# Decode attention: K turned by VectorE in 32 by 32 squares of bf16 pairs, products 512 columns wide, one quad of heads per loop turn

## The chip, the cores and the metric

The kernel runs on one core of a Trainium2 chip. The metric is the device time of one execution in microseconds (us). The profile's span, from the first to the last instruction, is about 1.8 us shorter than the time. Engines are called as in the profile: PE is TensorE (PEld its weight loads), DVE is VectorE, ACT is ScalarE, POOL is GpSimd, SP is the engine that issues transfers (SPq its queue). "The clock" is the one granted to TensorE, as a part of the full one.

Here "slow" means over 1.5% above the fastest run of the same kernel. Comparisons below use fast runs, except where a slow one is named as such.

## The reference, cut to what matters

One token goes through attention over a cache of 4096 positions and then a gated MLP. All tensors are bf16.

```python
Hq, Hkv, Sk, Dh = 32, 32, 4096, 128      # every head has its own K and V
q = x_norm @ wq                          # 640 -> 32 x 128
scores = einsum("bhqd,bhkd->bhqk", q, k) * Dh ** -0.5
p = softmax(scores)
o = einsum("bhqk,bhkd->bhqd", p, v) @ wo # 4096 -> 640
h = x + o
h2 = h + (gelu(n @ w_gate) * (n @ w_up)) @ w_down   # n = layernorm(h), 640 -> 1728 -> 640
```

K and V have 33.5 MB each; with the weights, 84.23 MB are read from HBM once per execution. Nothing is used twice.

## The kernel before

Four heads make a quad; a quad's K, and its V, is one tile of 128 partitions (4 heads x 32 rows) by 128 positions by 128 features, 4 MB. The kernel wants the features on the partitions for its score products, so TensorE transposes the 128 blocks of a K tile into PSUM, and VectorE and ScalarE copy them back over K. Then come 128 score products with four columns each, the exponentials, and 128 pv products with four columns each. Two tiles of K and two of V are kept, so a load waits for the use of two quads back. (The parts from several places; cuts are marked.)

```python
def pe_transposes(slot, mark, after):
    ...
        for b in range(GRP):                       # 8 blocks to a PSUM bank
            inst = PE.transpose(tp_b[g % NBANK][:, b*DH:(b+1)*DH], kt[slot][:, g*GRP+b, :], ident[:])
    ...
def pe_scores(slot, half, ready, mark):
    for j in range(half * NB // 2, (half + 1) * NB // 2):
        ...
        inst = PE.matmul(s_ps[half][:, j % (NB // 2), :], lhsT=kt[slot][:, j, :],
                         rhs=q8[:, slot*QH:(slot+1)*QH], start=True, stop=True)
    ...
def pe_pv(slot, half, mark):
    landed(f"v{slot}{'ab'[half]}")
    ...
        inst = PE.matmul(o_ps, lhsT=vt[slot][:, j, :], rhs=e_t[:, j, :], start=(j == 0), stop=(j == NB - 1))
    ...
def load_v(m):
    load_kv("v", m, vt, A_v_cache, m >= SLOTS and pe_at(m - SLOTS, "pv"))
...
for m in range(NQ):                                # the order of transfers
    load_k(m)                                      # the last K in two halves
    if m in (0, 2, 4):
        load_wo(m // 2)
    ...
    load_v(m)
load_wo(TURNS - 1)                                 # last part of wo: after the last V
load("wg", ...); load("wu", ...)                   # then w_down
```

The softmax here doesn't subtract the row's maximum and nothing guards it: scores larger than these inputs give would overflow.

## Time and profile before

| | before |
|---|---|
| time, median of 6 runs | 207.52 us (206.64 to 207.79) |
| span of the profiled run | 205.6 us |
| bytes, share of the transfer engines' span | 84.23 MB, 96.2% |
| PE, DVE, ACT busy | 72%, 36%, 40% |

These are lines of the profile's page: the span, the busy time of each engine with its share and its count of instructions, then the transfers' share in 40 equal slices (tenths, 9 is 90% or more), then the transfer queue with its packets, megabytes and share.

```profile
span 205.6 us, 7384 instructions
...
PE 148.5 (72%) x3409; PEld 138.2 (67%) x3409; DVE 73.6 (36%) x185; ACT 81.5 (40%) x179; POOL 19.1 (9%) x17
...
DMA  7999999999999999999999999999999999999980
...
q1 hardware_dynamic: 3952, 84.23, 96.2%
```

The transfer row is full from the second slice to the last but two, while no engine is busy more than 72% of the time. So transfers set the pace. Only at the end do they stop before the program does: at about 200 us of 205.6.

The chain of waits that ended last, followed back from the last instruction, tells what the end consists of. Its columns are start in us, length in us, and what ran.

```profile
171.35 0.87 PE tp_103 L252 x8
...
186.28 1.87 PE o L278 x64
188.15 0.54 PE tp_106 L300 x2
...
200.25 2.39 PE tp_105 L437 x54
...
202.66 0.33 DVE y_row L682
```

The last quad's transposes start at 171.35, its pv ends at 188.15 (186.28 + 1.87), and the rest of the program takes 17.45 us more. No transfer is in the chain.

The groups of instructions give durations from which the change could be costed: line, engine, operation, names, shape and count, then busy us and mean ns of one, then the idle time before them.

```profile
L278 PE MATMUL o<-ex,big 128*128 128x4 bf16 x1024 | 29.9, 166 | 10.2 <-ACT ex L567 6.3 <-issue 3.9
...
L252 PE MATMUL tp_103<-ident,big 128*128 128x128 bf16 x256 | 25.0, 256 | 11.9 <-PEq L176 11.9
...
L580 DVE COPY big<-tp_106 128x1024 bf16<-128x1024 bf16 x24 | 16.6, 691 | 2.9 <-PE tp_106 L252 2.4
...
L643 DVE STREAM_TRANSPOSE g_col<-tp_103 128x416 f32<-128x416 f32 x1 | 0.6, 605 | 0.0
```

The last of these lines: a DVE transpose of 416 f32 elements per partition takes 0.605 us.

### The profile page before, as it was taken

How to read it: one execution, taken by the hardware profiler on the slowest of the kernel's cores; microseconds unless marked ns; L12 is line 12 of the kernel's file. 1: busy time of each engine (PE TensorE's matmuls, PEld its weight loads, DVE VectorE, ACT ScalarE, POOL GpSimd, SP SyncE). 2: the span in 40 equal slices, each digit the busy share in tenths (PEclk: the TensorE clock that was granted, in tenths of full speed). 3: DMA queues.
4: the chain of work that ended last, by engine and by line, in shares of the span. 5: the costliest groups of instructions: out<-in, count | busy, mean ns of one | idle time of the engine just before them, and what ended most of it. 6: DMA issues, size and time to landing. Idle time of an engine off the chain costs nothing. (4 is left out here: it accounts for less than half of the span.)

```text
span 205.6 us, 7384 instructions
## 1 busy us (share of the span) xinstructions
PE 148.5 (72%) x3409; PEld 138.2 (67%) x3409; DVE 73.6 (36%) x185; ACT 81.5 (40%) x179; POOL 19.1 (9%) x17
## 2 busy tenths in 40 slices
PE   0001859955996499869986997099859989986654
PEld 0000259855996499869986997099759979986422
DVE  4006127400570058005701830058016703842570
ACT  0000136540476138614670755037704671772000
POOL 8200000530000000800000053000000000000000
PEclk9999979955595559955955995569856985995555
DMA  7999999999999999999999999999999999999980
GB/s 255 406 454 414 404 457 424 451 434 411 418 446 403 440 424 446 427 434 414 459 427 414 440 421 434 427 453 421 434 421 453 392 427 456 418 426 430 377 327 1
DMA packets 3963, 84.39 MB, mean 410 GB/s; under 512 B 464, under 2 KB 464, under 8 KB 752
## 3 DMA queue, kind: packets, MB, share of 16 engines
q1 hardware_dynamic: 3952, 84.23, 96.2%
q8 instruction: 8, 0.13, 0.3%
q14 instruction: 3, 0.02, 0.0%
HBM read 84.23 MB, written 0.00 MB: 410 GB/s over the span
## 5 line engine op out<-in xcount | busy, mean ns | idle before, releaser
L278 PE MATMUL o<-ex,big 128*128 128x4 bf16 x1024 | 29.9, 166 | 10.2 <-ACT ex L567 6.3
L278 PEld LDWEIGHTS o<-ex,big 128*128 128x128 bf16 x1024 | 28.5, 103 | 11.5 <-ACT ex L567 7.5
L553 ACT COPY big<-tp_104 128x1024 bf16<-128x1024 bf16 x16 | 16.2, 1012 | 47.8 <-PE tp_104 L252 47.8
L252 PE MATMUL tp_103<-ident,big 128*128 128x128 bf16 x256 | 25.0, 256 | 11.9 <-PEq L176 11.9
L252 PEld LDWEIGHTS tp_103<-ident,big 128*128 128x128 bf16 x256 | 20.4, 118 | 12.4 <-issue 12.4
L252 PE MATMUL tp_104<-ident,big 128*128 128x128 bf16 x256 | 24.4, 251 | 0.0
L580 DVE COPY big<-tp_103 128x1024 bf16<-128x1024 bf16 x24 | 16.5, 688 | 19.6 <-PE tp_103 L252 19.6
L252 PE MATMUL tp_105<-ident,big 128*128 128x128 bf16 x256 | 23.3, 244 | 0.0
L500 POOL COPY wo<-wo_in 128x5120 bf16<-128x5120 bf16 x3 | 13.3, 4449 | 104.8 <-PE a L288 104.8
L252 PE MATMUL tp_106<-ident,big 128*128 128x128 bf16 x256 | 22.7, 240 | 0.0
L252 PEld LDWEIGHTS tp_104<-ident,big 128*128 128x128 bf16 x256 | 20.0, 116 | 0.0
L252 PEld LDWEIGHTS tp_105<-ident,big 128*128 128x128 bf16 x256 | 19.1, 112 | 0.0
L252 PEld LDWEIGHTS tp_106<-ident,big 128*128 128x128 bf16 x256 | 18.7, 110 | 0.0
L265 PE MATMUL sb<-q_77,big 128*128 128x4 bf16 x512 | 14.4, 165 | 4.6 <-issue 4.6
L580 DVE COPY big<-tp_106 128x1024 bf16<-128x1024 bf16 x24 | 16.6, 691 | 2.9 <-PE tp_106 L252 2.4
L553 ACT COPY big<-tp_105 128x1024 bf16<-128x1024 bf16 x16 | 16.2, 1014 | 3.2 <-PE tp_105 L252 3.2
L265 PEld LDWEIGHTS sb<-q_77,big 128*128 128x128 bf16 x512 | 13.7, 97 | 4.8 <-issue 4.8
L567 ACT ACTIVATE ex<-sa 32x64 bf16<-32x64 f32 x32 | 9.8, 305 | 11.4 <-PE sa L265 11.2
L580 DVE COPY big<-tp_105 128x1024 bf16<-128x1024 bf16 x16 | 11.1, 692 | 8.4 <-PE tp_105 L252 8.1
L265 PE MATMUL sa<-q_77,big 128*128 128x4 bf16 x512 | 14.0, 165 | 0.0
L265 PEld LDWEIGHTS sa<-q_77,big 128*128 128x128 bf16 x512 | 13.5, 95 | 0.6
L637 DVE COPY o_raw<-o 128x4 f32<-128x4 f32 x4 | 0.6, 162 | 35.8 <-PE o L278 35.8
(111 smaller groups left out, 112.8 us busy)
## 6 DMA issues: line engine op xcount, KB each, us to landing
big<-in_A_v_cache_dram SPq DMA_DIRECT2D x8, 4096.0 KB, 33.7
big<-in_A_k_cache_dram SPq DMA_DIRECT2D x7, 4096.0 KB, 25.9
big<-in_A_wq_dram SPq DMA_DIRECT2D x1, 5120.0 KB, 15.1
wo_in<-in_A_wo_dram SPq DMA_DIRECT2D x4, 1280.0 KB, 27.0
big<-in_A_k_cache_dram SPq DMA_DIRECT2D x2, 2048.0 KB, 23.7
big<-in_B_w_gate_dram SPq DMA_DIRECT2D x1, 2160.0 KB, 38.8
big<-in_B_w_up_dram SPq DMA_DIRECT2D x1, 2160.0 KB, 44.0
big<-in_B_w_down_dram SPq DMA_DIRECT2D x1, 1280.0 KB, 31.9
```

The lines of the kernel that those rows point to most:

```text
L252: inst = PE.transpose(tp_b[g % NBANK][:, b * DH : (b + 1) * DH], kt[slot][:, g * GRP + b, :], ident[:])
L265: inst = PE.matmul(s_ps[half][:, j % (NB // 2), :], lhsT=kt[slot][:, j, :], rhs=q8[:, slot * QH : (slot + 1) * QH], start=True, stop=True,)
L278: inst = PE.matmul(o_ps, lhsT=vt[slot][:, j, :], rhs=e_t[:, j, :], start=(j == 0), stop=(j == NB - 1))
L500: POOL.tensor_copy(wo_t[:], wo_in[:]).then_inc(S["wo"], 1)
L553: ACT.copy(group(m % SLOTS, g), tp_g[g % NBANK]).then_inc(S["act_pe"], 1)
L567: inst = ACT.activation(e_t[r, cols, i], s_ps[half][r, :, i], AF.Exp, scale=SCALE, accum_out=rs_all[r, half, h : h + 1])
L580: DVE.tensor_copy(group(m % SLOTS, g), tp_g[g % NBANK]).then_inc(S["dve_pe"], 1)
L637: event(DVE.tensor_copy(o_raw[:, HG * turn : HG * turn + QH], o_ps))
```

## The change

Its intent is to take the transposes from TensorE, with their 16 PSUM copies per quad, and to replace many narrow products by few wide ones. VectorE turns K in squares of 32 by 32 elements, and the elements are f32 words, so each carries a pair of bf16. Afterwards the even and odd features of a pair are one word apart, and a score product reads every second bf16 of the turned tile. The query becomes the stationary operand, spread so that one of four heads is hit per group of rows; 32 products of 512 columns give all scores of a quad in one bank. pv also has 512 columns, four products side by side, and four f32 products gather the four results.

The program around it changes too: there are two raw K tiles, one turned K tile and *one* V tile; a loop turn is one quad and finishes it, projection included; the last part of wo is loaded before the last K; the last K comes whole. The core of the diff (cuts marked):

```diff
-    kt = [tile_at(i) for i in range(SLOTS)]
-    vt = [tile_at(SLOTS + i) for i in range(SLOTS)]
+    kr = [part(i * TILE, TILE) for i in range(SLOTS)]
+    vt = part(SLOTS * TILE, TILE).rearrange("p (j d) -> p j d", d=DH)
+    kt = part((SLOTS + 1) * TILE, TILE)
 ...
+    def pe_scores(mark):
+        for c in range(NC):
+            PE.wait_ge(S["kt"], c + 1)
+            for k in range(2):
+                for e in range(2):
+                    ...
+                        lhsT=q_wide[:, 2 * k + e, NC - 1 - c : NC - 1 - c + P],
+                        rhs=kt_at[:, k, c, :, e],
 ...
+    with nc.Fori(0, NQ, engines=(only_pe,)):
+        mark = mark_at("quad")
+        pe_scores(mark)
+        PE.wait_ge(S["act_pe"], 1)
+        pe_totals(t_ps, mark)
+        landed("v")
+        pe_pv(mark)
+        PE.wait_ge(S["act_pe"], 2)
+        pe_outputs(mark)
+        ...
+        pe_project(mark)
 ...
     def load_v(m):
-        load_kv("v", m, vt, A_v_cache, m >= SLOTS and pe_at(m - SLOTS, "pv"))
+        if m > 0:
+            SP.wait_ge(S["pe"], pe_at(m - 1, "pv"))
+        load("v", vt.rearrange("p j d -> p (j d)"), rows_of(A_v_cache, m))
 ...
     for m in range(NQ):
         load_k(m)
-        if m in (0, 2, 4):
+        if m % 2 == 0:
             load_wo(m // 2)
         load_v(m)
-    load_wo(TURNS - 1)
 ...
+    for m in range(NQ):                        # VectorE
+        ...                                    # wait for K of this quad
+        for c in range(NC):
+            DVE.transpose(to[:, c], of[:, c].rearrange("p (j k n) -> p j k n", k=2, n=HP)).then_inc(S["kt"], 1)
+        wait_pe(pe_at(m, "s"))
+        ... DVE.transpose(s_turned[:].rearrange("p j c -> p (j c)"), s_bank[:])
+        ...                                    # wait for totals, outputs, reorder
+        DVE.tensor_copy(o_row[:], r_ps).then_inc(S["dve_pe"], 1)
```

## The prediction

> **What bounds the kernel now.** Transfers. The profile's queue table gives one queue 84.23 MB and 96.2% of the span; the windows view shows about 430 GB/s at a share of 1.00 from 5 to 195 us. Transfers start at about 1.5 us and fade out at 200 us; 5 us of computation follow. The engines have slack in the stream (page: PE 72%, DVE 36%, ACT 40%). The bytes stay, so the change lifts no bound; it can only expose computation. The end is already compute: in the chain of waits, pv of the last quad ends at 188.15 and 17.4 us follow.
>
> **What the change removes.** Per quad 128 PE transposes (0.85 us for 8 at clock 0.5, 0.45 at 1.0), 16 PSUM copies (0.69 us DVE, 1.01 us ACT), and 256 products 4 wide. PE busy should fall to about 90 us, ACT to about 30.
>
> **What it adds, per quad.**
> - Eight DVE transposes of 128x1024 f32. The timeline has 416 elements in 0.61 us and 64 in 0.21, back to back 0.73[...].
> - 32 score products 512 wide. The query products, 512 wide and four side by side, take 0.427 us a group at the cold clock; warm I take 0.215.[...]. So PE catches up with DVE and ends about 1.2 us after it.
> - One 0.71 us score transpose, four exponentials of 0.36+0.20 us (2.4), totals 0.55, pv in 8 groups 1.7 to 3.4, ACT copy 0.59, four f32 products (about 1.5), then o_col, spread, reorder, o_row, q_to (about 1.2).
>
> **What it moves.** These steps run in series: DVE starts the next K only after o_row. Serial period, estimate: 20.6 us (19.8 to 22). Transfers need 19.5 us a quad, 22.5 with wo: mean 21.0. Nearly equal. V has one buffer: its next load waits for pv, about 17.1 us after K transposes start, while 19.5 us of transfers are queued, so gaps stay small.
> - Start: queries are ready at 27.7, three memsets (1.1 us) and q_to come before the first transpose, at about 29.0. First pv ends at 46.2, when K1 has landed (46.0): a gap of about 1.3 us.
> - End: the wo load now comes before the last K, which lands at about 173.5. From there 17.1 us to pv's end, then about 19 us (17.4 as before plus 1.6 for copy and f32 products): 209.7. From the compute side: 29.0 + 7x20.6 + 17.1 + 19 = 209.3.
>
> Both give a span near 209.6; the time is 1.9 us above the span. I add 1 us for lags that do not overlap: 212.5 us, +2.4%. Range 208.5 to 220. Chances: faster 0.02, same 0.41, slower 0.57.
>
> **What would show it.** K transposes 1.1 to 1.3 us each; pv to pv about 21 us; DMA share still 1.0 in most slices, a gap near 47 us; clock 0.5 early in the scores, then 1.0; no wait for transfers in the last 36 us of the chain, which runs DVE transposes, scores, exp, pv, outputs, then the MLP; transfers done 5 us or more before the end.
>
> **What would make it wrong.** DVE transposes from SBUF at half rate (9 us more per quad: near 275 us). PE staying cold through the scores (4.6 us per quad: near 240). The exponential slow on its strided SBUF source.[...]

Where a cut is marked, the forecast had words that no trace bears out. With them goes the term of the eight transposes, put at 9.3 us in all: an estimate that no trace showed. The sums still hold it: with 1.2 us to the end of the scores, 0.71 for the score transpose, 2.4 for the exponentials and 0.55 for the totals it makes 14.2 us, and with 2.9 for pv the 17.1 us from K to pv's end. The serial period of 20.6 us and the span of 209.6 us rest on it too, and so does the claim that PE catches up with DVE.

## The result, and the profile after

| | before, same rounds | after |
|---|---|---|
| time, median of all runs | 207.30 us (206.21 to 208.01, 20 runs) | 211.97 us (209.12 to 215.59, 10 runs) |
| ratio of fast runs | | 1.0157 (95% interval 1.0119 to 1.0195) |
| span of the profiled run, fast | 205.6 us | 207.5 us |

The ratio is the mean time of one kernel's fast runs over that of the other's fast runs of the same rounds, so it is not quite the ratio of the medians. It says 1.6%, about 3.3 us, slower: clear of noise, but inside the 2% within which two kernels count as the same here. The median of all runs is higher because four of the ten timed runs, at 214.3 to 215.6 us, count as slow. The profiled run, 209.35 us, is one of the quicker ones.

The page of the kernel after, the same lines as before:

```profile
span 207.5 us, 2498 instructions
...
PE 127.9 (62%) x1010; PEld 58.0 (28%) x1010; DVE 102.6 (49%) x192; ACT 23.0 (11%) x75; POOL 19.1 (9%) x16
...
DMA  7999999999999999999999999999999999999940
...
q1 hardware_dynamic: 3808, 84.23, 95.5%
```

Instructions fell from 7384 to 2498, and ACT and PE have less to do. The transfer row is as full as before, and the bytes are the same. What grew is the piece after the transfers.

The chain that ended last, after (start, length, what ran):

```profile
174.97 1.26 DVE big L539
...
176.27 9.43 PE s L247 x32
...
186.47 0.51 ACT ex L489 x2
...
188.97 1.86 PE pv L262 x32
...
190.86 0.59 ACT pv_sb L498
...
191.50 1.07 PE o L274 x8
...
203.08 1.43 PE y L378 x60
...
204.54 0.32 DVE y_row L581
```

It starts with the transposes of the last K at 174.97 and goes through scores, exponentials, pv, copy, f32 products and projection to the MLP: 32.5 us to the end of the span, one step after another. The timeline (start, length, instruction, and in brackets the idle time before it with what ended it) says why it starts there:

```profile
174.97 9.13 DVE L539 STREAM_TRANSPOSE big<-big 128x1024 f32<-128x1024 f32 x8 [1.62 <-DVEq L535]
```

"DVEq" is VectorE's own queue, waiting on a semaphore. By the program this is the one that the last K's landing raises, and the view of transfers agrees: K was issued at 151.65 and landed 23.2 us later, at 174.9. In all, VectorE waited for K in five of eight quads:

```profile
DVE big L539 <- DVEq L535: 9.4, 5, 3.8
```

The groups, after:

```profile
L247 PE MATMUL s<-big,q_wide 128*128 128x512 bf16 x256 | 74.7, 459 | 17.4 <-DVE big L539 17.2
L539 DVE STREAM_TRANSPOSE big<-big 128x1024 f32<-128x1024 f32 x64 | 73.0, 1208 | 9.4 <-DVEq L535 9.4
...
L262 PE MATMUL pv<-big,ex 128*16 128x512 bf16 x256 | 19.4, 457 | 0.0
...
L274 PE MATMUL o<-of_row,pv_sb 128*128 128x4 f32 x64 | 10.9, 293 | 5.5 <-ACT pv_sb L498 5.5
```

Eight transposes take 9.13 us per quad in the timeline, 1.13 us from one start to the next. They free TensorE and ScalarE, but those were not what the time depended on.

### The profile page after: what moved, and what is told of

It reads as the page before. It is cut to its first block, busy times and chain, and to the rows that moved or that the text cites. A ratio compares the mean times of both kernels' runs of the same rounds, so it can differ in the third digit from the quotient of the medians.

```text
span 207.5 us, 2498 instructions
## 1 busy us (share of the span) xinstructions
PE 127.9 (62%) x1010; PEld 58.0 (28%) x1010; DVE 102.6 (49%) x192; ACT 23.0 (11%) x75; POOL 19.1 (9%) x16
## 3 DMA queue, kind: packets, MB, share of 16 engines
q1 hardware_dynamic: 3808, 84.23, 95.5%
## 5 line engine op out<-in xcount | busy, mean ns | idle before, releaser
L247 PE MATMUL s<-big,q_wide 128*128 128x512 bf16 x256 | 74.7, 459 | 17.4 <-DVE big L539 17.2
L539 DVE STREAM_TRANSPOSE big<-big 128x1024 f32<-128x1024 f32 x64 | 73.0, 1208 | 9.4 <-DVEq L535 9.4
L247 PEld LDWEIGHTS s<-big,q_wide 128*128 128x128 bf16 x256 | 27.7, 112 | 63.0 <-DVE big L539 24.0
L489 ACT ACTIVATE ex<-s_turned 32x128 bf16<-32x128 f32 x32 | 15.6, 487 | 121.1 <-DVE o_col L542 120.8
L262 PE MATMUL pv<-big,ex 128*16 128x512 bf16 x256 | 19.4, 457 | 0.0
L298 PE MATMUL t<-rs_cur,ones_f 128*128 128x4 f32 x16 | 3.5, 288 | 23.2 <-ACT ex L489 23.2
L274 PE MATMUL o<-of_row,pv_sb 128*128 128x4 f32 x64 | 10.9, 293 | 5.5 <-ACT pv_sb L498 5.5
L274 PEld LDWEIGHTS o<-of_row,pv_sb 128*128 128x128 f32 x64 | 10.2, 242 | 10.8 <-ACT pv_sb L498 10.8
L308 PE MATMUL o<-x_col,mean_f 128*128 128x10 f32 x2 | 0.6, 376 | 16.4 <-DVE x_col L204 16.4
L286 PE MATMUL a<-wo,o_row 128*1 128x160 bf16 x256 | 7.8, 281 | 2.1 <-DVE o_row L550 2.1
L262 PEld LDWEIGHTS pv<-big,ex 128*16 128x16 bf16 x256 | 6.4, 99 | 8.0 <-issue 3.9
L498 ACT COPY pv_sb<-pv 128x512 f32<-128x512 f32 x8 | 4.7, 586 | 23.2 <-PE pv L262 23.2
L489 ACT ACTIVATION_READ_ACCUMULATOR ex<-s_turned 32x1 f32 x32 | 5.9, 184 | 0.0
L308 PEld LDWEIGHTS o<-x_col,mean_f 128*128 128x128 f32 x2 | 0.5, 310 | 16.4 <-DVE x_col L204 16.4
```

Of the source, the lines that this page charges most:

```text
L247: inst = PE.matmul(s_bank[:], lhsT=q_wide[:, 2 * k + e, NC - 1 - c : NC - 1 - c + P], rhs=kt_at[:, k, c, :, e], start=first, stop=last,)
L262: inst = PE.matmul(pv_bank[32 * r : 32 * r + VG * QH, :], lhsT=e_t[:, j : j + VG, :].rearrange("p j h -> p (j h)"), rhs=vt[:, j : j + VG, ...
L274: inst = PE.matmul(o_ps, lhsT=pv_sb[:, i * DH : (i + 1) * DH], rhs=of_row[:, i * QH : (i + 1) * QH], start=i == 0, stop=i == VG - 1,)
L286: inst = PE.matmul(attn_ps[32 * r : 32 * r + 1, :], lhsT=o_row[:, j : j + 1], rhs=wo_t[:, j, r * YW : (r + 1) * YW], start=False, stop=j = ...
L298: mark("totals", PE.matmul(ps, lhsT=ones_f[:], rhs=rs_cur[:], start=True, stop=True))
L489: inst = ACT.activation(e_t[r, :, i].rearrange("p (c j) -> p c j", c=NC), s_turned[r, :, 0:NC].rearrange("p j c -> p c j"), AF.Exp, scale= ...
```

## The experiments

The theory after the result: both kernels stream at the transfers' pace; the change costs time because the chain after the last K (or V) is longer and starts later. Call it the tail theory. Its rivals were that the single V buffer stops the transfers, that the serial chain sets the pace of the whole stream, that a later K alone costs the time, and that VectorE's transposes as such do. The clock was a side question: in the trace of the changed kernel it was 1.00 during the last pv and 0.50 during the third, and the runs spread. Twelve kernels were run. The record marks all twelve results as correct, that of e_half too, although it leaves out half of the score products; so the check of results does not notice that loss.

### The changed kernel once more (e_control)

> The changed kernel itself, again, to learn how its times spread beside the variants of the same call. Its first ten timed runs lay in three clumps, near 209.4, 212 and 215.4 us, at granted clocks of 0.795, 0.79 and 0.77. All theories expect the same picture: 209 to 216 us, median near 212.

It had a median of 211.65 us (209.91 to 215.65, six runs), and a ratio of 1.0174 (1.0136 to 1.0213). The result repeats, with two slow runs again.

### Half the work per quad (e_half)

```diff
-        for c in range(NC):
+        for c in range(HALF):        # HALF = NC // 2, for transposes and for score products
```

> Wrong result on purpose: only the first four of eight K chunks are turned and multiplied in each quad, which takes 4.6 us of VectorE and about the same of TensorE out of every quad, 37 us in all. Tail theory: the stream stays at the transfers' pace, the last K lands at 175 us as before, and only the 4.6 us of the last quad are gained: 204.5 to 206.5 us. Theory that the serial chain sets the pace of the whole stream: the last K lands several microseconds earlier than 175.

Measured: 208.34 us median (206.07 to 210.63, four runs), ratio 1.0088 (1.0039 to 1.0137). The timeline of the last quad in its trace:

```profile
175.09 4.62 DVE L541 STREAM_TRANSPOSE big<-big 128x1024 f32<-128x1024 f32 x4 [3.28 <-DVEq L537]
181.76 0.72 DVE L543 STREAM_TRANSPOSE s_turned<-s 128x512 f32<-128x512 f32 x1 [2.04 <-PE s L249]
```

VectorE waited 3.28 us for the last K instead of 1.62, and K came at 175.09 instead of 174.97. Taking about 4.6 us of work out of each of eight quads did not bring the last K earlier at all. So the stream is not paced by the serial chain; only the last quad's share counts. The win was smaller than the 4.6 us expected, and three of the four runs lay above the expected 204.5 to 206.5 us. By the ratios of fast runs beside the control's (1.0088 and 1.0174) it was about 1.8 us; between the two profiled spans it was 3.3 us (207.5 to 204.2), but the profiled run of e_half was the fastest of its four. The kernel with half the transposes is still 0.9% slower than the kernel before. From the first transpose to the score transpose it was 4.1 us (6.67 instead of 10.75), and 0.7 us were lost again in the MLP.

### Two buffers for V (e_v2)

```diff
-        if m > 0:
-            SP.wait_ge(S["pe"], pe_at(m - 1, "pv"))
 ...
+        if m == 0:
+            SP.wait_ge(S["q"], 1)
+        if m > 1:
+            SP.wait_ge(S["pe"], pe_at(m - 2, "pv"))
 ...
+    SP.wait_ge(S["pe"], pe_at(NQ - 2, "pv"))
     load("wg", wg_sb, B_w_gate.rearrange("(p c) f -> p c f", c=DC))
```

The second buffer lies in the space of the MLP weights, so the first V now waits for the queries and the MLP weights for pv of the last quad but one.

> V gets two buffers (the one for even quads in the space of the MLP weights), so its loads wait for pv of two quads back; two quads per loop turn for that. Buffer theory: no load of V is ever held up, so the runs above 211 vanish and all lie near 209. Tail theory: transfers were hardly held up at all, so the fast level stays at 209.4 and the clumps at 212 and 215 stay too.

Measured: 210.96 us median (209.64 to 214.06), ratio 1.0149 (1.0109 to 1.0189), beside 1.0174 of the control in the same rounds. In its trace VectorE starts on the last K at 175.23, and runs near 212 and 214 us stayed. The single V buffer does not explain the loss, although the changed kernel waits for it from the second V on: the transfers' share in the changed kernel's trace is 0.99 to 1.01 in each stretch of 20 us from 20 to 180, so the wait ends before the queued transfers run out.

### The last K in halves (e_k7half)

```diff
+        if m == NQ - 1:
+            h = TILE // 2
+            load(f"k{m % SLOTS}", kr[m % SLOTS][:, 0:h], rows_of(A_k_cache, m)[:, 0:h])
+            load("k7b", kr[m % SLOTS][:, h:], rows_of(A_k_cache, m)[:, h:])
```

> One thing undone: the last K comes in two halves, as in the kernel before, and VectorE may turn its first four chunks when the first half is there. In the trace of the changed kernel VectorE waits 1.6 us for the last K (1.3 us in the trace of a slow run). Tail theory: at most this wait is won, 0.5 to 1.6 us, and the clumps stay: 208 to 214.5 us, median near 210.5. Theory that late transfers make the difference: the last K's first half lands 5 us earlier, so up to 4 us are won.

Measured: 209.61 us median (209.02 to 211.60), ratio 1.0169 (1.0130 to 1.0207). By the ratio nothing was won. Its timeline shows why an earlier K does not help here:

```profile
173.87 0.16 DVE L554 TENSOR_TENSOR o_col<-o,rinv 128x4 bf16<-128x4 f32 x1 [5.90 <-PE o L274]
...
174.87 9.13 DVE L547 STREAM_TRANSPOSE big<-big 128x1024 f32<-128x1024 f32 x8
```

No wait for K stands before these transposes, and the first half had landed at 170.6: VectorE came from the sixth quad's output (counted from zero), whose o_col began 1 us earlier. The serial chain of one quad and the landing of the next K are so close to each other that taking one away can uncover the other. In this one trace the chain was a long one: the sixth quad's pv took 3.59 us, where the changed kernel's trace has 1.90.

### wo before the last K in the kernel before (e_before_wo)

```diff
-        if m in (0, 2, 4):
+        if m in (0, 2, 4, 6):
 ...
-    load_wo(TURNS - 1)
```

> The kernel before, with one part of the change: the last 1.31 MB of wo are loaded before the last K and not after the last V. Its last K, in two halves, lands 3 us later, at about 170 and 175.5 us, and its TensorE begins the last quad at 171.3 and needs the second half at 175.9. Tail theory: just in time, so 0 to 2 us slower (206.5 to 209). If the later last K is by itself what the change costs, 3 us slower (210).

Measured: 207.77 us median (206.96 to 207.97), ratio 1.0033 (1.0000 to 1.0066). The later last K alone, which this order of loads brings, costs the kernel before at most 0.7%. There TensorE was still at work on the quad before when K landed: in the trace of e_before_wo the halves landed at 170.4 and 175.4, and the transposes began at 171.31 (in the first profile 167.3, 172.2 and 171.35). The loss needs the new, longer chain as well.

### Idle products to keep the clock up (e_warm, e_warm20, e_tailwarm)

These add products into a bank that nobody reads: 12 beside the exponentials of every quad, and 8 or 20 after the projection; the third has 12 before and 12 after the last quad's scores, and 3 and 10 in the end.

```diff
+    def pe_warm(n):
+        for _ in range(n):
+            PE.matmul(t_bank[:], lhsT=warm[:, 0:P], rhs=warm[:], start=True, stop=True)
 ...                                   # and the calls, as told above
```

> TensorE is kept busy with products that nobody reads: 12 of 512 columns while the exponentials run, 8 after the output projection. Tail theory (transfers set the pace of the stream; the added time is the serial chain after the last K has landed, and the clumps come from TensorE being at half clock in the scores and pv of that chain): the granted clock rises above 0.9, every pv takes 1.9 us instead of 1.9 to 3.6, the clumps at 212 and 215 vanish, and all runs lie within 208 to 210. Buffer theory (the clumps come from transfers held up by the single V buffer): pv ends earlier too, so the clumps may shrink, but the two-buffer run decides. Clock-does-not-matter theory: the spread stays, 209 to 216.

> As the first run with idle products, but 20 instead of 8 after the output projection, since in that run the clock still fell to half where VectorE waited 4.2 us for K, which included the last quad. Clock theory: no quad starts its scores at half clock any more, the scores end 1.0 us after the last transpose in every quad, the chain after the last K is 32 us, and all runs lie within 208.5 to 210 us. If the tail's length is not the clock's doing, the runs spread from 209 to 215 as in the control.

> Idle products only around the last quad, which is unrolled for that: 12 before its scores (VectorE waits 1 to 4 us for K there), 12 while its exponentials run, 3 and 10 in gaps of the end. Quads 0 to 6 are untouched. Clock theory of the tail: scores end 10.3 us after the last quad's first transpose, 6.9 us from the score transpose to the last o_col (9.6 in the slow trace of the control), under 15 us from there to the end; so the tail from the last K is 31.5 to 32.5 us and the time 208 to 210, apart from runs whose last K lands late. If the runs still spread over 209 to 215.5, the spread comes from before the last quad.

Measured: e_warm 211.78 us (210.58 to 212.09), ratio 1.0200 (1.0171 to 1.0229), clock 0.91 to 0.92; e_warm20 214.90 us (212.46 to 218.51), ratio 1.0347 (1.0297 to 1.0396), clock 0.94 to 0.97; e_tailwarm 211.46 us (210.12 to 211.77), ratio 1.0195 (1.0155 to 1.0234). So all three failed as repairs: e_warm and e_tailwarm had been expected within 208 to 210 us, and none of their twelve runs was. With the highest clock of all, e_warm20 is the slowest, and the expectation that it would bring all runs to 208.5 to 210 us was wrong. The trace of e_tailwarm shows how idle products cost time. Its timeline around the last quad:

```profile
175.09 9.13 DVE L554 STREAM_TRANSPOSE big<-big 128x1024 f32<-128x1024 f32 x8 [0.48 <-DVEq L550]
175.68 0.13 PEld L242 LDWEIGHTS t<-warm 128*128 128x128 bf16 x2 [0.27 <-issue]
...
180.41 7.38 PE L252 MATMUL s<-big,q_wide 128*128 128x512 bf16 x32
...
187.82 0.72 DVE L556 STREAM_TRANSPOSE s_turned<-s 128x512 f32<-128x512 f32 x1 [3.60 <-PE s L252]
```

The 12 idle products took 4.89 us, where the 12 behind the scores took 2.75 in the same trace, and the real scores behind them began 5.3 us after the first transpose. The score transpose began 12.73 us after the first transpose, where the changed kernel needed 10.75 us. Here the real scores had to wait for the idle products in front of them.

### The query write before the memsets (e_noclash)

In the trace of e_warm20, which is that of a slow run (218.51 us), one small instruction stood out. The timeline:

```profile
29.15 4.45 POOL L447 COPY wo<-wo_in 128x5120 bf16<-128x5120 bf16 x1 [26.51 <-POOLq L444]
29.25 4.44 DVE L535 TENSOR_TENSOR q_wide<-q_turned,of_head 128x16 bf16<-128x16 bf16 x1
```

The write of the widened query, 0.23 us in the other traces, took 4.44 us, as long as POOL's copy of wo that began 0.1 us before it. That the copy held the write up is the author's reading of this one trace. In the other traces of kernels with this write it began 0.1 to 1.7 us before the copy and took 0.23 us, so the next experiment moved it ahead of the memsets.

```diff
-    for ps in (g_ps, u_ps, y_ps):
-        dve(lambda: DVE.memset(ps, 0.0), False)
 ...
+        if m == 0:                     # after q_wide of the first quad
+            for ps in (g_ps, u_ps, y_ps):
+                dve(lambda: DVE.memset(ps, 0.0), False)
```

> In one trace the first write of the widened query, with two inputs in SBUF, took 4.44 us instead of 0.23: it started 0.1 us after GpSimd's copy of wo. In the other traces it ends only 0.2 to 1.1 us before that copy starts. Here it is done before the three PSUM memsets, 1.1 us earlier. Clash theory: the runs at 214 to 215.6 us of the unchanged kernel are those in which it was hit, so they vanish: all 209 to 212.5. Clock theory: they stay, about one run in three.

Measured: 210.54 us median (209.07 to 215.56), ratio 1.0142 (1.0095 to 1.0189). Two of six runs were slow again, at 215.12 and 215.56, so the clash is not what makes the slow runs. The slow run in the trace of e_control (214.17 us) had no clash either: its write took 0.23 us.

### K one quad ahead, scores before pv (e_pipe, e_joint)

The repair that the tail theory asks for: load K one quad ahead of V and do the next quad's scores before this quad's pv, so that only the last V's work is left at the end. The second of these also loads the last wo after the last V and projects the last two quads together.

```diff
-        pe_scores(mark)                # scores(m), then pv(m)
+        if ahead:
+            pe_scores(mark)            # scores(m+1), then pv(m)
 ...
-        load_k(m)
+        if m + 1 < NQ:
+            load_k(m + 1)
```

> A repair: K is loaded one quad ahead of V, and TensorE and VectorE do the scores of the next quad before pv of this one. Nothing else changes. Tail theory: the last V, at about 185 us, starts the tail instead of the last K at 175 us; pv and what follows took 18.5 us in the trace of the changed kernel, so the span is 203.5 to 206.5 us, depending on the clock, and the time 205.5 to 208.5. A theory in which VectorE's transposes as such cost the time (its load is the same here) expects no gain over 209 to 215.

> The repair, and the last two quads are projected together from the landed weights, as in the kernel before, so that the last 1.31 MB of wo are loaded after the last V instead of before. The last V lands 3 us earlier, at about 182 us. Tail theory: another 1 to 3 us less than the repair alone; the end of the transfers at 200 us plus the 3.5 to 5 us for the last product and the store becomes the bound: 204 to 206.5 us.

Measured: e_pipe 213.96 us (212.00 to 214.58), ratio 1.0330 (1.0286 to 1.0374); e_joint 212.42 us (212.02 to 213.36), ratio 1.0289 (1.0264 to 1.0314). Both were slower than the changed kernel, against the expectation. Three views of e_pipe tell where the win went. TensorE's timeline:

```profile
166.49 10.04 PE L247 MATMUL s<-big,q_wide 128*128 128x512 bf16 x31 [7.50 <-DVE big L550]
...
176.57 1.90 PE L262 MATMUL pv<-big,ex 128*16 128x512 bf16 x32
...
190.76 3.59 PE L262 MATMUL pv<-big,ex 128*16 128x512 bf16 x32 [8.47 <-PEq L169]
```

The sixth quad's pv now stands behind the last scores and ends at 178.5. SP's timeline shows the last V issued just then, as there is one V buffer:

```profile
178.52 0.33 SPq L454 DMA_DIRECT2D big<-in_A_v_cache_dram  x1
```

And the windows view shows the gap. It lists for each stretch its length, the busy time of PE, PEld, DVE, ACT and POOL with counts, the clock, the transfers' share and their GB/s:

```profile
165.00:170.00 5.00, 3.51 (x9) 1.30 (x10) 4.81 (x5) 0.00 (x0) 0.00 (x0) 0.50 0.97 419
170.00:175.00 5.00, 4.95 (x18) 1.93 (x18) 4.31 (x4) 0.00 (x0) 0.00 (x0) 0.79 0.53 229
175.00:180.00 5.00, 4.30 (x48) 2.40 (x47) 0.83 (x3) 1.43 (x5) 0.00 (x0) 1.00 0.36 98
```

Transfers fell to 229 and then 98 GB/s for ten microseconds, since behind the last V stood the MLP weights and nothing was queued before it. The last V's pv began at 190.76, no earlier than in the changed kernel (188.9). In e_joint the same wait left the queue empty for longer: 3 GB/s from 170 to 175. A dependence that was harmless in one order, pv to the next V load, had become the bound in another.

### The repair with the gap closed (e_best)

Here the last V goes into the first K tile, which is free early, and w_down into V's tile; the rest is e_joint with the early query write and 35 idle products in the end.

```diff
+    vt7 = part(0, TILE).rearrange("p (j d) -> p j d", d=DH)
 ...
+        if m == NQ - 1:
+            SP.wait_ge(S["dve"], D_SCORES[NQ - SLOTS])
+            to = vt7
```

> The repair again, without what spoiled it: in its trace the load of the last V waited until 178.9 us for pv of the quad before, which now came after the next scores, and the transfers fell to 216 and 99 GB/s in two slices. Here the last V goes into the first K buffer, free since 154 us, and w_down into V's; the query write comes early as in the other run, and idle products fill the end. Tail theory with transfers as the only other bound: no gap, the last V lands at about 182 us, transfers end at about 200, and the span ends 4 us after them: 204 us, a time of 205 to 207. If it stays above 209, something else than the order of loads and the serial chain costs the time.

Measured: 207.18 us median (206.14 to 208.24), a little above the expected 205 to 207, ratio to the kernel before 1.0007 (0.9964 to 1.0049). The same stretches of the windows view show the transfers without the deep gap:

```profile
165.00:170.00 5.00, 5.00 (x16) 1.80 (x15) 5.00 (x5) 0.00 (x0) 0.00 (x0) 0.62 1.04 446
170.00:175.00 5.00, 5.00 (x46) 2.35 (x48) 2.24 (x4) 0.00 (x0) 0.00 (x0) 1.00 1.00 433
175.00:180.00 5.00, 3.26 (x23) 1.76 (x16) 0.16 (x1) 2.62 (x9) 0.00 (x0) 0.91 0.90 381
```

The chain that ended last now leads back to a transfer:

```profile
157.32 38.31 DMA big<-in_B_w_up_dram
...
195.68 2.16 PE u L430 x15
197.83 3.13 PE t L244 x10
200.96 1.36 PE y L413 x60
```

The up projection waits for w_up, which landed at 195.6, 38.31 us after its issue. This version has the same eight transposes per quad on VectorE as the changed kernel, and it takes no longer than the kernel before. So the transposes as such are not what the change cost. What it cost was where the serial chain stood at the end of the stream. (The parts of this version were not taken away one by one, so their shares are not known. But the early query write alone (1.0142), idle products alone (1.0195 and more) and the new order with the gap (1.0289) did not win back the loss. The ten idle products after the up projection ended at 200.96, while the values for the last product were ready at 199.6; without them about 1.3 us might be won. That was not run.)

### The tails, side by side

From the timelines: the first transpose of the last K; us from there to the score transpose; from that to the last o_col; from that to the end of the span. All traces are of fast runs.

| kernel | last K's transposes begin | to score transpose | to o_col | to the end | span |
|---|---|---|---|---|---|
| changed | 174.97 | 10.75 | 6.87 | 14.9 | 207.5 |
| e_half | 175.09 | 6.67 | 6.86 | 15.6 | 204.2 |
| e_k7half | 174.87 | 10.66 | 6.86 | 14.9 | 207.3 |
| e_noclash | 176.02 | 10.68 | 6.87 | 14.9 | 208.5 |
| e_v2 | 175.23 | 10.30 | 8.40 | 16.4 | 210.3 |
| e_warm | 175.69 | 11.54 | 6.87 | 16.1 | 210.2 |
| e_tailwarm | 175.09 | 12.73 | 6.89 | 15.3 | 210.0 |

The first column moves by 1.2 us. The three that follow sum to 29.1 us in e_half, 32.4 to 32.5 in the changed kernel, e_k7half and e_noclash, and 34.5 to 35.1 in e_v2, e_warm and e_tailwarm: the spans differ mostly by their tails. Part of this is the clock. In the changed kernel's trace pv took 1.90 us where the clock was 1.00 and 3.59 where it was 0.50, the f32 products 1.06 or 1.87. Which of them falls into a half-clock stretch differs from trace to trace.

## Why the prediction was right

It said 212.5 us with a range of 208.5 to 220; the median of all runs was 211.97. It gave "slower by over 2%" the larger chance; the fast runs' ratio is 1.0157, below its +2.4%, and its interval does not reach 2%. So the nearness of 211.97 to 212.5 is in part luck: the median holds four slow runs (that of the six other timed runs is 209.97), and in the fast trace two terms that were too long outweighed a K that was said to land too early. The mechanism, a longer serial tail under an unchanged stream, is what held. Point by point:

- **Transfers bound both.** Right, and shown: a share of 1.00 from 5 to 195 us in both traces, and half the work per quad left the last K's landing where it was.
- **Eight transposes, 9.3 us in all** (estimate). Measured 9.13, 1.13 us from one start to the next. The group view gives 1.208 us each because neighbours overlap.
- **Scores end about 1.2 us after the last transpose.** Measured: the wait between the last transpose and the score transpose is 1.17 to 2.08 us, 1.62 in the last quad. The clock was 0.50 early in these scores and then 1.0, as said: in the last quad it rose about 4.3 us after the first product. In the trace before it rose 2.8 to 5.3 us after the first of a quad's transposes; the 3.8 us of the prediction are those of the last quad (171.35 to 175.15). That the query products ran at the "cold" clock was the inference from their 0.427 us a group, and its 0.215 for a warm one is about half of that; the windows view gives the clock there as 1.00. Groups of pv, of the same width, took 0.24 us at 1.00 and 0.45 at 0.50 in the trace after (1.90 and 3.59 us for eight).
- **Exponentials 2.4, pv 1.7 to 3.4, f32 products 1.5.** Measured 2.1, 1.9 to 3.6, and 1.06 or 1.87.
- **Serial period 20.6 (19.8 to 22).** The two quads that did not wait for K took 19.8 and 21.8 us from transpose to transpose. The first, without its wait, needed about 18.6, and the mean of all seven without their waits is 19.6, one below the prediction. From pv to pv it was 20.95 on average, as said (about 21), because VectorE waited for K in between.
- **From K to pv's end 17.1 us.** Mis-sized by 1.2: the last quad took 15.9 (174.97 to 190.84). The terms of the forecast without pv, the 9.3 us of the transposes among them, add up to 14.2 us, and 14.0 were measured; so 17.1 leaves 2.9 for pv, which took 1.86 at the full clock.
- **After pv about 19 us.** Mis-sized: 16.7 (190.84 to 207.5). The clock was full where it had been half before: the last product took 1.43 us instead of 2.39, the attention projection 0.75 instead of 1.26. And the totals with their reciprocal, which stood behind pv before (0.54 and 0.22), were done beside it. These two terms, less the 1.5 us by which K came later than said, are why the profiled span is 207.5 and not 209.6.
- **A gap of 1.3 us near 47 us.** Wrong in the profiled run. The first pv ended at 44.1, not 46.2, and the second K landed at 49.0, not 46.0, so the next V was issued in time. But what the prediction feared shows in the slow trace of e_control: the first pv took 3.59 us instead of 1.90, the next V was issued at 47.29 instead of 44.18, and the transfers' share fell to 0.70 from 45 to 50.
- **The last K at 173.5.** It landed at 174.9.
- **The chain in the end.** Right, name by name, with no transfer in its last 32 us.
- **Busy time.** ACT fell to 23 us (said: about 30), but PE only to 128 (said: about 90). Products 512 wide are recorded with a mean of 459 ns each and overlap, and they often ran at the half clock (its mean was 0.795), so the count of columns is a poor guide to this number.

What stays open: what puts some runs of the changed kernel above 214 us. None of the 12 runs of e_warm and e_tailwarm was there, and two of six of e_noclash were, but idle products change more than the clock, and the one slow trace of the changed kernel is a single run. That trace shows two of its parts, the gap near 47 us named above, after which the last K's transposes began at 176.43, and a last pv of 3.59 us again; whether the other slow runs are like it is not known.

## What to carry to other kernels

In this kernel, paced by transfers, work taken off the engines in the middle of the stream won nothing; what counted was the serial chain that starts when the last K lands. So in a kernel of this kind look at which load is last, which step waits for it, and what can still be in flight behind it. Before reordering work, list what each step releases: pv moved behind the next scores also moved the load that waited for it, and the transfers stopped. Products added only to keep a clock up stood in front of the real ones here, 4.89 us of them in e_tailwarm, and won nothing in three tries.

## What else the traces show

- In the changed kernel a VectorE transpose of 1024 f32 elements per partition took 1.13 us from start to start, 1.1 ns for each element. As each f32 word carries a pair of bf16, that is 128 x 2048 bf16 per 1.13 us.
- In the kernel before the clock fell from 1.0 to 0.5 while PE was busy with products four columns wide, 1.68 of 2 us, with gaps of at most 0.6 us between them, as these stretches of its windows view show:

```profile
165.00:167.00 2.00, 1.77 (x71) 1.68 (x67) 0.00 (x0) 1.73 (x7) 0.00 (x0) 1.00 0.96 410
...
169.00:171.00 2.00, 1.68 (x63) 1.60 (x60) 0.00 (x0) 0.42 (x2) 0.00 (x0) 0.50 1.19 508
```

- Idle products raised the mean clock from about 0.80 to 0.91 and more in every run of e_warm and won no time: ratio 1.0200 beside 1.0174.
- The gap of e_pipe shows little in its queue's average share. The profile page of e_pipe has the queue at 93.2%, that of the changed kernel at 95.5%; it is the windows view that shows ten microseconds at 229 and 98 GB/s.
